# z's norms taken by four rows from slots of their own, and z's statistics, scalings, block sums and w_sp's pieces moved to other chunks

## The chip, the cores and the metric

One core of a Trainium2 chip runs the whole kernel. The metric is the device time of one execution in microseconds (us), as the median of several. Engines are named as in the profile: PE is TensorE's matmul, PEld its weight load, DVE is VectorE, ACT is ScalarE, POOL is GpSimd, SP is SyncE, which only issues transfers (SPq).

## The reference

An FNet layer (two DFTs) and a gMLP layer, each behind a layer norm with a shift, a scale and a gate from `c`. S = 2048 rows, D = 512, half width Fh = 896.

```python
mod = (_silu(c) @ w_mod).reshape(c.shape[0], 6, 1, -1)
sa, ca, ga, sb, cb, gb = (mod[:, 0], ..., mod[:, 5])
h = _layernorm(x) * (1 + ca) + sa
x = x + ga * _A_ref(h, ...)         # y = Re(DFT_seq(DFT_hidden(h)))
h = _layernorm(x) * (1 + cb) + sb
z = _gelu(einsum("bsd,df->bsf", h, w_in))
z1 = z[..., :Fh]
z2 = _layernorm(z[..., Fh:])
g = einsum("ts,bsf->btf", w_sp, z2) + b_sp[None, :, None]
x = x + gb * einsum("bsf,fd->bsd", z1 * g, w_out)
```

## The kernel before

**Arithmetic.** Every fp32 product is made of three matmuls (`matmul3`, L96 to L98): each operand is split into a high part (ACT copies it to fp32r: `ah`, `bh`, `wh`) and a low part (DVE subtracts: `al`, `bl`, `wl`). The large products are done with seven block products instead of eight (the "forms" 1, 2, 6, 7, 4, 5, 3), so sums of blocks of `w_in`, of h and of `w_sp` are made on DVE, and partial results are copied between PSUM banks and SBUF on ACT, or added on DVE, when a form is finished.

**Chunks.** PE's work is a list of chunks, and everything else hangs on their numbers. Five stages matter here; "y+3" is chunk 3 of stage y.

- **y** (`Y0`, 32 chunks of 12 matmuls): the last FNet product. Per row block m, `load_g` brings `gr` from DRAM (SP), `split_g` makes `gh` (ACT, L91) and `gl` (DVE, L92), `seed_y` writes x into the PSUM bank (ACT, L856), `post_y` copies the result out as `x` (ACT, L868), stores it (POOL, `x_d`) and takes its norm; `norm_y` and `post_h` make h and store it (POOL, `h_d`, L880). The tile of `x` has two slots, that of `gr` two.
- **z1** (`N2`, which is also `YE`; 28 chunks, 16 of 12 matmuls and 12 of 9): the left half of z, forms in the order above, two chunks to a form, once for each half of the rows.
- **z2** (`N3`, 28 chunks of 12 matmuls of 448 columns): the right half of z. The first 14 chunks give rows 0 to 7 (of 16 blocks of 128 rows, called rows from here on), the last 14 rows 8 to 15 (`zq`). When form 6, 7, 2 or 4 is done, ACT copies (L1037) or applies gelu (L1039); after forms 5 and 3, DVE adds (L1042) and ACT applies gelu (L1046). Form 3 goes on in the banks that form 5's adds read, and form 7 in those that form 6's copies read, so PE waits for these at once.
- **gw** (`N4`, `NB[p]`): seven products with `w_sp`, 16 chunks each, in the order 1, 6, 7, 4, 5, 3, 2; then the last product, **o**.

**What sets the order.** `at(n, f, ...)` and `atd` enter a call into a table under chunk n; `run(n)` emits what stands there, in order of entry: in y behind the chunk's matmuls, in z1 and z2 ahead of them (and behind `prep(n)`, which makes `al` for chunk n + 2, L272, and `ah` for n + 3, L264), in gw behind them. There is no scheduler: an engine runs its instructions in this order, and one that waits holds up all behind it. SP is not tied to chunks in time, only in order: it issues a load as soon as its slot is free.

**What the change touches.** `stat_z` takes the statistics of one half of a row (DVE, L1059); `norm_z` joins the two halves (DVE, L1063) and takes the reciprocal root and the shift on POOL (L1065 to L1068), in tiles `mvz`, `rsz`, `nmrz` of which there are four slots each; `scale_z` applies them, on DVE for rows 4 to 7 (L1074), on ACT for all others (L120, called from L1076). `hi_w`, `lo_w`, `sum_w` split and sum the blocks of `w_in`'s right half for z2. The 16 pieces of `w_sp` whose block sums are taken ahead: `load_s` brings one (SP, 768 KB in two transfers), `sum_s` makes three sums (DVE, L1099, L1100, L1103), and these go to `s_d` (three stores of 256 KB, by POOL, or in stage y by SP through `store_s`, L1111). `sum_t23(k)` sums blocks of the scaled z (DVE, L1134, L1135) for form 6 of gw.

Of the kernel before, what the change touches and what calls it, by code (L numbers as in the profile page):

```python
# [19 lines left out]
def fnet_gmlp_kernel(  # L20
# [91 lines left out]
    def norm(src, name):
# [902 lines left out]
    def mm_z2(n):  # L1015
        i, c = divmod(n - N3, NP)
        q, p, k = 1 - i, FORMS[c // 2], c % 2
        here, there = (0, 4) if i == 0 else (4, 0)
# [4 lines left out]
        th, tl = AH.pop(n), AL.pop(n)
        wh, wl = WF[1, p]
        for r in range(4):
            ts = slice(r * P, (r + 1) * P)
            matmul3(acc[r][:, :ZH], th[:, ts], tl[:, ts], wh[:, k], wl[:, k], k == 0 and p in (1, 5), k == 1, p not in (1, 5))
        if k == 0:
            return
        ta, tb = [4 * TS[2 * q + j] for j in range(2)]  # L1030
        left, right = slice(0, ZH), slice(ZH, FH)
        for r in range(4):
            if p == 1:
                ZG[r] = bank(there + r, f"z2g{q}_{r}")
                nc.scalar.activation(ZG[r][:, :ZH], ZT[r][:, :ZH], AF.Copy)
            elif p in (6, 7):
                nc.scalar.activation(row_z((ta if p == 6 else tb) + r)[:, right], ZG[r][:, :ZH], AF.Copy)  # L1037
            elif p in (2, 4):
                nc.scalar.activation(row_z((ta if p == 2 else tb) + r)[:, left], acc[r][:, :ZH], AF.Gelu_apprx_tanh)  # L1039
            else:  # L1040
                z = Z[(tb if p == 5 else ta) + r][:, right]
                nc.vector.tensor_tensor(z, ZT[r][:, :ZH], z, op=ALU.add)  # L1042
# [12 lines left out]
    def stat_z(s, h):
        g = s // 8
# [2 lines left out]
        nc.vector.bn_stats(ST[g][:, s % 8, h, :6], Z[s][:, h * ZH:(h + 1) * ZH])  # L1059

    def norm_z(s):
        mv = small.tile([P, 2], F32, tag="mv", name=f"mvz{s}")
        nc.vector.bn_aggr(mv, ST[s // 8][:, s % 8, :, :6])  # L1063
        r = small.tile([P, 1], F32, tag="rs", name=f"rsz{s}")
        nc.gpsimd.tensor_scalar(mv[:, 1:2], mv[:, 1:2], EPS, 1.0, op0=ALU.add, op1=ALU.mult)  # L1065
        nc.gpsimd.tensor_tensor(r, mv[:, 1:2], mhalf, op=ALU.pow)
        nmr = small.tile([P, 1], F32, tag="nmr", name=f"nmrz{s}")
        nc.gpsimd.tensor_scalar(nmr, mv[:, 0:1], r, -1.0, op0=ALU.mult, op1=ALU.mult)  # L1068
# [610 lines left out]
```

## Time and profile before

| | us |
|---|---|
| median of 3 runs (lowest, highest) | 931.78 (931.55, 932.77) |
| the profiled execution | 932.23 |
| its span, first to last instruction | 930.4 |
| PE busy | 917.4 (99%) |
| DVE busy | 759.1 (82%) |
| ACT busy | 447.3 (48%) |
| POOL busy | 153.0 (16%) |
| mean granted TensorE clock | 0.998 |

How to read it: the page gives each engine's busy time and the groups of instructions; the view of waits says which engine waited for which instruction, how long in total, how often, and the longest; a timeline row gives start, duration, engine, line, operation and, in brackets, how long the engine had stood idle and what ended that; windows give an engine's busy time in a stretch, the clock granted to PE and the busy share of the 16 DMA engines. In the profiled execution stage y starts at 343.24 us, z1 at 432.64, z2 at 501.62 and gw at 577.72.

### The profile page before, as it was taken

The numbers are of one execution on the slowest core, as the hardware profiler recorded it, in microseconds if no ns is written. First come the engines' busy times: TensorE is split into PE (matmuls) and PEld (weight loads), VectorE is DVE, ScalarE is ACT, GpSimd is POOL, SyncE is SP. The second block draws the span as 40 slices with busy tenths as digits, with TensorE's granted clock in tenths as the row PEclk, the third lists the DMA queues.
The fourth block names the chain that finished last, engine by engine and source line by source line (L and its number), as shares of the span: only waits on it lengthen the run. The fifth ranks groups of instructions, "written<-read, shape, count | busy, mean of one in ns | idle before, by whom it ended". The sixth has DMA issues, their size and how long they took to land.

```text
span 930.4 us, 12042 instructions
## 1 busy us (share of the span) xinstructions
PE 917.4 (99%) x4040; PEld 759.3 (82%) x4040; DVE 759.1 (82%) x1039; ACT 447.3 (48%) x721; POOL 153.0 (16%) x291
## 2 busy tenths in 40 slices
PE   9999999999999999999999989999999999999998
PEld 6888888888888888877888978888888888888886
DVE  7879789889978885978786877986799789895972
ACT  3585354354354354555777665653554444431221
POOL 1431001100110015745121151500100100000000
PEclk9999999999999999999999999999999999999999
DMA  9999948798864658995783354768878856742641
GB/s 207 225 204 190 223 107 228 190 170 193 226 188 107 181 180 243 339 288 188 228 299 147 118 121 131 219 159 234 218 183 255 220 117 146 192 127 102 210 152 56
DMA packets 261310, 174.62 MB, mean 188 GB/s; under 512 B 134720, under 2 KB 225088, under 8 KB 261120
## 3 DMA queue, kind: packets, MB, share of 16 engines
q1 hardware_dynamic: 246592, 132.16, 57.3%
q0 software_dynamic: 11664, 39.08, 11.2%
q10 hardware_dynamic: 2992, 2.62, 1.2%
q8 instruction: 31, 0.51, 0.2%
q14 instruction: 31, 0.25, 0.1%
HBM read 130.81 MB, written 43.00 MB: 187 GB/s over the span
## 4 chain that ended last, share of the span: by engine, by line
PE 82%; DVE 6%; DMA 5%; issue 3%; ACT 2%; POOL 2%; SPq 0%; ACTq 0%; DVEq 0%; POOLq 0%
PE gw L97 9%; PE gw L98 9%; PE gw L96 9%; PE gs_c L97 3%; PE gs_c L98 3%; PE gs_c L96 3%; PE op L97 3%; PE op L96 3%; PE op L98 3%; PE gp L98 2%; PE gp L633 2%; PE gp L96 2%; PE gp L97 2%; PE gs_u L97 2%; PE gs_u L96 2%
## 5 line engine op out<-in xcount | busy, mean ns | idle before, releaser
L97 PE MATMUL gw<-al,bh 128*128 128x512 f32 x400 | 155.8, 390 | 0.3 <-DVE al L272 0.3
L98 PE MATMUL gw<-ah,bl 128*128 128x512 f32 x400 | 155.7, 389 | 0.0
L96 PE MATMUL gw<-ah,bh 128*128 128x512 f32 x400 | 155.6, 389 | 0.0
L264 ACT ACTIVATE ah<-t 128x512 fp32r<-128x512 f32 x120 | 75.0, 625 | 87.9 <-PE gw L98 46.7
L272 DVE TENSOR_TENSOR al<-t,ah 128x512 fp32r<-128x512 f32 x120 | 81.5, 686 | 37.3 <-PE gw L97 35.0
L97 PEld LDWEIGHTS gw<-al,bh 128*128 128x128 f32 x400 | 75.1, 188 | 16.7 <-DVE al L272 1.2
L98 PEld LDWEIGHTS gw<-ah,bl 128*128 128x128 f32 x400 | 75.1, 188 | 15.6
L96 PEld LDWEIGHTS gw<-ah,bh 128*128 128x128 f32 x400 | 75.1, 188 | 15.5
L231 DVE STREAM_TRANSPOSE t<-stage 128x1024 f32<-128x1024 f32 x56 | 69.4, 1239 | 2.5 <-DMA stage<-in_B_w_sp_dram 2.5
L602 ACT ACTIVATE ph<-f 128x1024 fp32r<-128x1024 f32 x42 | 44.4, 1058 | 40.7 <-PE gs_c L98 17.2
L606 DVE TENSOR_TENSOR pl<-f,ph 128x1024 fp32r<-128x1024 f32 x42 | 50.9, 1215 | 14.0 <-ACT ph L602 13.8
L97 PE MATMUL gs_c<-pl,hh 128*128 128x512 f32 x144 | 56.1, 390 | 0.1
L98 PE MATMUL gs_c<-ph,hl 128*128 128x512 f32 x144 | 56.1, 389 | 0.0
L96 PE MATMUL gs_c<-ph,hh 128*128 128x512 f32 x144 | 56.0, 389 | 0.0
L602 ACT ACTIVATE ph<-tp 128x1024 fp32r<-128x1024 f32 x35 | 36.9, 1054 | 38.3 <-PE gs_v L98 15.9
L606 DVE TENSOR_TENSOR pl<-tp,ph 128x1024 fp32r<-128x1024 f32 x35 | 42.2, 1207 | 7.2 <-ACT ph L602 7.2
L537 DVE STREAM_TRANSPOSE tp<-stage 128x1024 f32<-128x1024 f32 x36 | 44.2, 1230 | 0.2
L96 PE MATMUL op<-woh,uh 128*128 128x512 f32 x112 | 43.6, 389 | 0.0
L97 PE MATMUL op<-wol,uh 128*128 128x512 f32 x112 | 43.6, 389 | 0.0
L98 PE MATMUL op<-woh,ul 128*128 128x512 f32 x112 | 43.6, 389 | 0.0
L1147 ACT ACTIVATE bh<-z 128x512 fp32r<-128x512 f32 (+1 forms) x40 | 23.5, 588 | 40.6 <-PE gw L97 36.6
L1234 ACT ACTIVATE uh<-g 128x512 fp32r<-128x512 f32 x16 | 10.1, 630 | 61.1 <-PE op L97 57.4
(302 smaller groups left out, 2292.7 us busy)
## 6 DMA issues: line engine op xcount, KB each, us to landing
stage<-s_d SPq DMA_DIRECT2D x128, 128.0 KB, 3.0
stage<-in_A_dft_seq_re_dram SPq DMA_DIRECT2D x52, 256.0 KB, 6.5
stage<-in_B_w_sp_dram SPq DMA_DIRECT2D x96, 128.0 KB, 3.3
stage<-in_A_dft_seq_im_dram SPq DMA_DIRECT2D x44, 256.0 KB, 5.3
s_d<-sj POOLq DMA_DIRECT2D x39, 256.0 KB, 3.6
sj<-in_B_w_sp_dram SPq DMA_DIRECT2D x16, 512.0 KB, 6.0
gr<-g_d SPq DMA_DIRECT2D x12, 512.0 KB, 6.8
sb<-in_A_dft_seq_im_dram SPq DMA_DIRECT2D x16, 256.0 KB, 6.0
```

The costliest lines, as they stand in the source:

```text
L96: nc.tensor.matmul(acc, ah, bh, start=first, stop=False, skip_group_check=go_on)
L97: nc.tensor.matmul(acc, ah, bl, start=False, stop=False, skip_group_check=go_on)
L98: nc.tensor.matmul(acc, al, bh, start=False, stop=last, skip_group_check=go_on)
L231: nc.vector.transpose(t.rearrange("p r (b i) -> p r b i", i=32), st[:, :, :, 16 * k:16 * k + 32])
L264: nc.scalar.activation(*parts_z(n, AH), AF.Copy)
L272: nc.vector.tensor_tensor(lo, src_, parts_z(n, AH)[0].bitcast(F32), op=ALU.subtract)
L537: nc.vector.transpose(dst.rearrange("p k (b i) -> p k b i", i=32), st[:, :, 64 * m:64 * m + 64].rearrange("p b (k i) -> p k b i", k=2))
L602: nc.scalar.activation(pair_of(PH, u, "ph"), source_unit(u), AF.Copy)
L606: nc.vector.tensor_tensor(pair_of(PL, u, "pl"), source_unit(u), PH[u].bitcast(F32), op=ALU.subtract)
L633: nc.tensor.matmul(GP[j, k], a[:, k, :], b, start=s == 0 and b is ah and a is h_hi[s], stop=False)
L1147: nc.scalar.activation(BH[p, k][:, :w], b_of(p, k), AF.Copy)
L1234: nc.scalar.activation(UT[t, i][0][:, :4], a, AF.Copy)
```

## The change

No matmul is added, removed or moved. Six things are different:

1. `norm_z` takes four rows at a time. Its tile of four rows by four numbers (mean, variance, root, shift) has the tag `bst`, with four slots, so each of the four groups has its own. Per group there are four joins on DVE, as before, and four POOL instructions on 128x4 instead of twelve on 128x1; the shift is now a product and a negation.
2. `stat_z` runs at n + 3 and n + 4 behind its form's last chunk n (was n + 1, n + 2), except form 2's, which stays in the first half and goes to n + 2, n + 3 in the second; `norm_z` at n + 5 (was n + 2, n + 3); `scale_z` from n + 7 (was n + 6 for rows 4 to 7 and n + 3 for the others).
3. `w_sp`'s pieces: of the three pieces in stage y the last goes to z1; the sums of the nine last pieces run at z1+15, z1+17, z1+21, z2+0, z2+2, z2+7, z2+9, z2+21 and z2+22 (were y+13, z1+15, z1+18, z2+7, z2+9, z2+19, z2+22, gw+2 and gw+5).
4. The sums and splits of `w_in`'s right half run one to three chunks later, from z1+22 on.
5. `sum_t23(k)` runs five chunks later, at gw+8+2k.
6. `mhalf` has four columns.

```diff
     def norm_z(s):
-        mv = small.tile([P, 2], F32, tag="mv", name=f"mvz{s}")
-        nc.vector.bn_aggr(mv, ST[s // 8][:, s % 8, :, :6])
-        r = small.tile([P, 1], F32, tag="rs", name=f"rsz{s}")
-        nc.gpsimd.tensor_scalar(mv[:, 1:2], mv[:, 1:2], EPS, 1.0, op0=ALU.add, op1=ALU.mult)
-        nc.gpsimd.tensor_tensor(r, mv[:, 1:2], mhalf, op=ALU.pow)
-        nmr = small.tile([P, 1], F32, tag="nmr", name=f"nmrz{s}")
-        nc.gpsimd.tensor_scalar(nmr, mv[:, 0:1], r, -1.0, op0=ALU.mult, op1=ALU.mult)
-        ZN[s] = r, nmr
+        m = small.tile([P, 4, 4], F32, tag="bst", name=f"mvz{s}")
+        for r in range(4):
+            nc.vector.bn_aggr(m[:, r, 0:2], ST[s // 8][:, (s + r) % 8, :, :6])
+            ZN[s + r] = m[:, r, 2:3], m[:, r, 3:4]
+        mean, var, rs, nmr = [m[:, :, j] for j in range(4)]
+        nc.gpsimd.tensor_scalar(var, var, EPS, 1.0, op0=ALU.add, op1=ALU.mult)
+        nc.gpsimd.tensor_tensor(rs, var, mhalf, op=ALU.pow)
+        nc.gpsimd.tensor_tensor(nmr, mean, rs, op=ALU.mult)
+        nc.gpsimd.tensor_scalar(nmr, nmr, -1.0, 1.0, op0=ALU.mult, op1=ALU.mult)
...
                 s_, h = (ta if p in (2, 3) else tb) + r, p in (5, 3)
-                at(n + 1 + r // 2, stat_z, s_, h)
+                at(n + (3 if p != 2 else 1 + i) + r // 2, stat_z, s_, h)
                 if h:
-                    at(n + 2 + r // 2, norm_z, s_)
-                    at(n + (3 if i or p == 3 else 6) + r, scale_z, s_, i == 0 and p == 5)
+                    at(n + 7 + r, scale_z, s_, i == 0 and p == 5)
+            if h:
+                at(n + 5, norm_z, s_ - 3)
...
-    early += tuple((Y0 + n, Y0 + m) for n, m in ((3, 6), (4, 8), (9, 13)))
-    early += tuple((YE + n, YE + m) for n, m in ((9, 15), (13, 18), (30, 35), (32, 37), (42, 47), (45, 50), (51, 58), (55, 61)))
+    early += tuple((Y0 + n, Y0 + m) for n, m in ((3, 6), (4, 8)))
+    early += tuple((YE + n, YE + m) for n, m in ((9, 15), (12, 17), (17, 21), (20, 28), (24, 30), (31, 35), (33, 37), (39, 49), (41, 50)))
...
-                     (18, (hi_w, 1, 2)), (19, (lo_w, 1, 2)), (20, (hi_w, 1, 1)), (21, (lo_w, 1, 1)), (22, (sum_w, 1, 5)),
-                     (23, (sum_w, 1, 6), (hi_w, 1, 6)), (24, (lo_w, 1, 6)), (25, (sum_w, 1, 7)), (26, (hi_w, 1, 7)), (27, (lo_w, 1, 7)),
-                     (28, (sum_w, 1, 4)), (29, (hi_w, 1, 4)), (30, (lo_w, 1, 4)), (31, (hi_w, 1, 5)), (32, (lo_w, 1, 5)), (33, (hi_w, 1, 3)),
-                     (34, (lo_w, 1, 3))):
+                     (18, (hi_w, 1, 2)), (19, (lo_w, 1, 2)), (20, (hi_w, 1, 1)), (22, (lo_w, 1, 1)), (23, (sum_w, 1, 5)),
+                     (24, (sum_w, 1, 6), (hi_w, 1, 6)), (26, (lo_w, 1, 6)), (27, (sum_w, 1, 7), (hi_w, 1, 7)), (29, (lo_w, 1, 7)),
+                     (31, (sum_w, 1, 4)), (32, (hi_w, 1, 4)), (33, (lo_w, 1, 4), (hi_w, 1, 5)), (34, (lo_w, 1, 5)), (35, (hi_w, 1, 3)),
+                     (36, (lo_w, 1, 3))):
...
-                at(n + 3, sum_t23, k)
+                at(n + 8, sum_t23, k)
```

Three places in the order of the instructions matter below. The first is ACT's order in the second half of z2, from form 1's copies (z2+15) to form 7's (z2+21); `ah` is a high part for PE, `zq` is z's rows 8 to 15, `z_0` to `z_3` are rows 0 to 3, and L120 is their scaling. Before:

```order
L1035 ACTIVATE z2g_3_4907<-z2p_1_3_4856 128x448
L264 ACTIVATE ah_4911<-hs_3763 128x4x4x32
L120 ACTIVATE z_0_4580<-z_0_4580,nmrz_4878,rsz_4875 128x896
L264 ACTIVATE ah_4942<-hz_3739 128x4x4x32
L120 ACTIVATE z_1_4582<-z_1_4582,nmrz_4885,rsz_4882 128x896
L1039 ACTIVATE zq<-z2p_1_0_4853 128x448
...
L264 ACTIVATE ah_4967<-hz_3739 128x4x4x32
L120 ACTIVATE z_2_4584<-z_2_4584,nmrz_4919,rsz_4916 128x896
L264 ACTIVATE ah_4997<-hz_3739 128x4x4x32
L120 ACTIVATE z_3_4586<-z_3_4586,nmrz_4926,rsz_4923 128x896
L1037 ACTIVATE zq<-z2g_0_4901 128x448
```

And now:

```order
L1035 ACTIVATE z2g_3_4882<-z2p_1_3_4845 128x448
L264 ACTIVATE ah_4886<-hs_3754 128x4x4x32
L264 ACTIVATE ah_4913<-hz_3730 128x4x4x32
L1039 ACTIVATE zq<-z2p_1_0_4842 128x448
...
L264 ACTIVATE ah_4935<-hz_3730 128x4x4x32
L264 ACTIVATE ah_4970<-hz_3730 128x4x4x32
L1037 ACTIVATE zq<-z2g_0_4876 128x448
...
L264 ACTIVATE ah_4994<-hz_3730 128x4x4x32
L120 ACTIVATE z_0_4592<-z_0_4592,mvz_4947 128x896
L264 ACTIVATE ah_5023<-hs_3751 128x4x4x32
L120 ACTIVATE z_1_4594<-z_1_4594,mvz_4947 128x896
```

The four scalings stood ahead of form 6's copies (L1037), two of them ahead of form 2's gelus (L1039); now the first stands behind form 6's copies.

The second place is DVE's order at the end of z1, about the adds of the second half's form 5 (L997, `z1k_7`; they free the banks in which form 3 goes on): `wl_6` is a low part of `w_in` for form 6 of z2, `wraw` the block sum for form 7. Before:

```order
L949 TENSOR_TENSOR wt_4387<-wraw_2_4167,wraw_0_4084 128x896
L272 TENSOR_TENSOR al_4410<-zq,ah_4385 128x512
L964 TENSOR_TENSOR wl_6_4390<-wt_4387,wh_6_4389 128x896
L272 TENSOR_TENSOR al_4427<-zq,ah_4412 128x512
L949 TENSOR_TENSOR wraw_0_4084<-wraw_2_4167,wraw_0_4084 128x2x448
L997 TENSOR_TENSOR z1k_7_0_4360<-z1p_5_0_4415,z1k_7_0_4360 128x512
```

And now:

```order
L949 TENSOR_TENSOR wt_4415<-wraw_2_4158,wraw_0_4075 128x896
L272 TENSOR_TENSOR al_4432<-zq,ah_4410 128x512
L997 TENSOR_TENSOR z1k_7_0_4360<-z1p_5_0_4420,z1k_7_0_4360 128x512
L997 TENSOR_TENSOR z1k_7_1_4362<-z1p_5_1_4421,z1k_7_1_4362 128x512
L997 TENSOR_TENSOR z1k_7_2_4364<-z1p_5_2_4422,z1k_7_2_4364 128x512
L272 TENSOR_TENSOR al_4454<-zq,ah_4434 128x4x4x32
L964 TENSOR_TENSOR wl_6_4418<-wt_4415,wh_6_4417 128x896
L272 TENSOR_TENSOR al_4468<-zq,ah_4456 128x4x4x32
L949 TENSOR_TENSOR wraw_0_4075<-wraw_2_4158,wraw_0_4075 128x2x448
```

`wl_6` and form 7's sum stood ahead of the adds and now stand behind them.

The third place is SP's queue in the second half of stage y: `sj` is a piece of `w_sp`, `stage<-h_d` the first load for z1. Before:

```order
L847 DMA xr_3397<-in_A_x_dram 128x512
L1111 DMA s_d_10_98<-sj_3238 128x512
L1111 DMA s_d_10_102<-sj_3238 128x512
L1111 DMA s_d_10_106<-sj_3238 128x512
L165 DMA stage_3419<-h_d_91 32x16x128 x4
L843 DMA gr_3427<-g_d_76 128x8x128
```

And now:

```order
L843 DMA gr_3360<-g_d_76 128x8x128
L847 DMA xr_3391<-in_A_x_dram 128x512
L165 DMA stage_3410<-h_d_91 32x16x128 x4
L843 DMA gr_3418<-g_d_76 128x8x128
L847 DMA xr_3448<-in_A_x_dram 128x512
```

The three stores of the third piece are gone from the queue ahead of `stage<-h_d` and the next `gr`, as are its two loads some rows earlier.

More of the change, by code (lines that the diff above doesn't have):

```diff
@@ L108, in stats @@
         nc.gpsimd.tensor_scalar(mv[:, 1:2], mv[:, 1:2], EPS, 1.0, op0=ALU.add, op1=ALU.mult)
-        nc.gpsimd.tensor_tensor(r, mv[:, 1:2], mhalf, op=ALU.pow)
+        nc.gpsimd.tensor_tensor(r, mv[:, 1:2], mhalf[:, 0:1], op=ALU.pow)
         return mv[:, 0:1], r
@@ L290, in fnet_gmlp_kernel @@
     ccol = cpool.tile([P, ND], F32, name="ccol")
-    mhalf = cpool.tile([P, 1], F32, name="mhalf")
+    mhalf = cpool.tile([P, 4], F32, name="mhalf")
     nc.gpsimd.memset(mhalf, -0.5)
@@ L404, in stats_first @@
         nc.vector.tensor_scalar(mv[:, 1:2], mv[:, 1:2], EPS, None, op0=ALU.add)
-        nc.gpsimd.tensor_tensor(mv[:, 2:3], mv[:, 1:2], mhalf, op=ALU.pow)
+        nc.gpsimd.tensor_tensor(mv[:, 2:3], mv[:, 1:2], mhalf[:, 0:1], op=ALU.pow)
         NRM[s] = mv[:, 0:1], mv[:, 2:3]
@@ L431, in square_x @@
         nc.gpsimd.tensor_scalar(m[:, 1:2], m[:, 1:2], 1.0 / D, EPS, op0=ALU.mult, op1=ALU.add)
-        nc.gpsimd.tensor_tensor(m[:, 2:3], m[:, 1:2], mhalf, op=ALU.pow)
+        nc.gpsimd.tensor_tensor(m[:, 2:3], m[:, 1:2], mhalf[:, 0:1], op=ALU.pow)
         nc.gpsimd.tensor_tensor(m[:, 3:4], m[:, 0:1], m[:, 2:3], op=ALU.mult)
@@ L1061, in norm_z @@
     def norm_z(s):
-        mv = small.tile([P, 2], F32, tag="mv", name=f"mvz{s}")
-        nc.vector.bn_aggr(mv, ST[s // 8][:, s % 8, :, :6])
-        r = small.tile([P, 1], F32, tag="rs", name=f"rsz{s}")
-        nc.gpsimd.tensor_scalar(mv[:, 1:2], mv[:, 1:2], EPS, 1.0, op0=ALU.add, op1=ALU.mult)
-        nc.gpsimd.tensor_tensor(r, mv[:, 1:2], mhalf, op=ALU.pow)
-        nmr = small.tile([P, 1], F32, tag="nmr", name=f"nmrz{s}")
-        nc.gpsimd.tensor_scalar(nmr, mv[:, 0:1], r, -1.0, op0=ALU.mult, op1=ALU.mult)
-        ZN[s] = r, nmr
+        m = small.tile([P, 4, 4], F32, tag="bst", name=f"mvz{s}")
[7 more added lines that the diff above has]
+        nc.gpsimd.tensor_scalar(nmr, nmr, -1.0, 1.0, op0=ALU.mult, op1=ALU.mult)
     def scale_z(s, on_vector):
@@ L1472, in load_gelu @@
     def load_gelu():
-        nc.scalar.activation(ccol[:, 0:1], mhalf, AF.Gelu_apprx_tanh)
+        nc.scalar.activation(ccol[:, 0:1], mhalf[:, 0:1], AF.Gelu_apprx_tanh)
     wstack = ctx.enter_context(ExitStack())
```

## The prediction

> **What bounds the kernel now.** First the page's line of busy times, then windows over the four stages that are edited (length, busy time and count of each engine, PEclk as the granted clock, DMA share), with one window from within stage y and one behind PE's longest wait.
>
> ```profile
> PE 917.4 (99%) x4040; PEld 759.3 (82%) x4040; DVE 759.1 (82%) x1039; ACT 447.3 (48%) x721; POOL 153.0 (16%) x291
> ```
>
> ```profile
> 343.20:432.60 89.40, 87.89 (x385) 71.86 (x384) 68.64 (x97) 46.41 (x66) 43.65 (x64) 1.00 0.86 262
> 432.60:501.60 69.00, 68.30 (x301) 56.25 (x301) 53.17 (x75) 48.54 (x82) 20.80 (x36) 1.00 0.75 252
> 501.60:577.70 76.10, 70.84 (x337) 64.07 (x336) 58.32 (x102) 51.59 (x93) 18.15 (x39) 0.98 0.37 113
> 577.70:665.30 87.60, 87.28 (x385) 71.95 (x385) 71.42 (x109) 44.90 (x73) 17.91 (x35) 1.00 0.77 209
> ...
> 379.00:391.00 12.00, 12.00 (x54) 9.94 (x54) 11.72 (x17) 6.55 (x9) 9.23 (x11) 1.00 1.05 367
> ...
> 555.30:558.80 3.50, 3.45 (x10) 3.09 (x10) 2.75 (x5) 1.82 (x4) 1.94 (x3) 0.52 0.35 144
> ```
>
> PE is the bound, and the matmuls stay the same, so only time that PE loses can be won. Where it is undisturbed (379 to 391), 53 matmuls start in 12.00 us (the window counts one more at its border), 0.2265 each: a chunk of twelve is 2.72 us, one of nine 2.04. Stage y should then last 32 x 2.72 = 87.0 and lasts 89.4 (2.4 lost); z1 16 x 2.72 + 12 x 2.04 = 68.0 of 69.0 (1.0 lost); gw's first two products 32 x 2.72 = 87.0 of 87.6 (0.6 lost). For z2 I take PE's timeline:
>
> ```profile
> 550.88 0.37 PE L98 MATMUL z2g<-wh,al 128*128 128x448 f32 x1
> 555.35 0.74 PE L96 MATMUL z2g<-wh,ah 128*128 128x448 f32 x1 [4.10 <-ACT zq L1037]
> ...
> 559.40 0.37 PE L96 MATMUL z2g<-wh,ah 128*128 128x448 f32 x1
> ...
> 561.84 0.36 PE L96 MATMUL z2g<-wh,ah 128*128 128x448 f32 x1
> ```
>
> The chunk z2+21, from 559.40 to 561.84, is undisturbed: 2.44. 28 x 2.44 = 68.3 of 76.1: 7.8 lost. Together **11.8 us** can be won, no more. PE's view of waits (us in total, times, longest) names the places:
>
> ```profile
> PE z2g L96 <- ACT zq L1037: 4.1, 1, 4.1
> PE yp L96 <- ACT yp L856: 1.5, 2, 0.8
> ...
> PE z2p L96 <- DVE zq L1042: 1.1, 1, 1.1
> PE z1p L96 <- DVE z1k L997: 0.7, 1, 0.7
> PE gw L97 <- DVE al L272: 0.3, 1, 0.3
> ```
>
> **The norms in z2: 5.9 us.** The timeline of the engines ahead of the long wait:
>
> ```profile
> 543.92 0.69 DVE L272 TENSOR_TENSOR al<-hs,ah 128x512 fp32r<-128x512 f32 x1 [1.14 <-PE z2p L98]
> 544.53 0.74 DVE L1074 TENSOR_SCALAR z<-z,rsz,nmrz 128x896 f32<-128x896 f32 x1
> ...
> 545.42 0.55 POOL L1066 TENSOR_TENSOR rsz<-mvz,mhalf 128x1 f32<-128x1 f32 x1 [2.61 <-DVE z L1074]
> ...
> 546.38 1.14 ACT L120 ACTIVATE z<-z,nmrz,rsz 128x896 f32<-128x896 f32 x1 [3.94 <-POOL nmrz L1068]
> ...
> 554.75 1.85 ACT L1037 ACTIVATE zq<-z2g 128x448 f32<-128x448 f32 x4
> 556.45 0.68 ACT L264 ACTIVATE ah<-hz 128x512 fp32r<-128x512 f32 x1
> ...
> 578.13 0.27 DVE L1063 BATCH_NORM_AGGREGATE mvz<-st 128x2 f32<-128x12 f32 x2
> ```
>
> `rsz` has four slots. The fifth row's root waits 2.61 on POOL until DVE has scaled the first row (L1074), which stands at z2+17 behind an `al` that itself waits for PE. ACT's scaling of `z_0` stands 3.94 behind that, and the gelus and copies behind it come late, so PE stands from 550.88 + 0.20 to 555.35 (4.3 lost); its next chunk takes 559.40 - 555.35 = 4.05 instead of 2.44 (1.6 more), at the granted clock 0.52 of the window from 555.3. With a slot per group no root waits for a scaling, and `z_0` to `z_3` stand behind form 6's copies: 5.9 gone. Late next is the new chain on POOL:
>
> ```profile
> L1066 POOL TENSOR_TENSOR rsz<-mvz,mhalf x16: 549/550/1000, 535.4 to 595.5; 128x1 f32<-128x1 f32 x16
> ...
> L1068 POOL TENSOR_SCALAR nmrz<-mvz,rsz x16: 267/268/804, 536.0 to 596.5; 128x1 f32<-128x1 f32 x16
> ...
> L1065 POOL TENSOR_SCALAR mvz<-mvz x16: 183/187/637, 535.1 to 594.8; 128x1 f32<-128x1 f32 x16
> ```
>
> (ns: least, median, most.) No row shows 128x4. At best four instructions cost medians: 0.19 + 0.55 + 0.27 + 0.27 = 1.3 us; at worst four times the slowest, 4 x (0.64 + 1.00 + 0.80 + 0.80) = 13.0. I take 1.3, the rows nearest in size. The room: DVE makes the four joins (0.54) at z2+18 behind `al` (0.69) and a scaling (0.74), so at 2.0 after that chunk's start. ACT runs form 6's copies from 0.6 into z2+19, when its first block is done, to 2.5, then an `ah` (0.68): it comes to `z_0` 0.7 into z2+20. Two scalings and an `ah` more (3.0) bring it to 1.3 into z2+21, and form 7's first copy (1.85 / 4) to 1.8 of 2.44: 0.6 to spare. 2 x 2.44 + 0.7 - 2.0 + 0.6 = 4.2 against 1.3: hidden.
>
> On the price of a rest: the rows show 1.6 us lost to the clock behind an idle of 4.3. In proportion, an idle of 2.2 would cost another 0.8. [...]
>
> **Form 5's adds: 1.4 us.** The same timeline, later:
>
> ```profile
> 562.72 0.68 DVE L1099 TENSOR_TENSOR sj<-sj 128x512 f32<-128x512 f32 x1
> ...
> 567.58 1.24 DVE L231 STREAM_TRANSPOSE t<-stage 128x1024 f32<-128x1024 f32 x1
> 568.74 0.65 DVE L1152 TENSOR_TENSOR bl<-z,bh 128x512 fp32r<-128x512 f32 x1
> ...
> 570.96 1.15 DVE L1059 BATCH_NORM_STATS2 st<-zq 128x6 f32<-128x448 f32 x2
> 572.02 2.20 DVE L1042 TENSOR_TENSOR zq<-z2p,zq 128x448 f32<-128x448 f32 x4
> ```
>
> Two pairs of statistics (1.15 each) stand ahead of the adds for which PE waits 1.1. They go behind, and at z2+25 DVE has only one `al` first: 1.1 gone. What is left of z2's loss, 7.8 - 5.9 - 1.1 = 0.8, has no row of its own; form 5's adds of the first half meet the same statistics, and I take 0.3 for them: 1.4 of 1.9.
>
> What they meet there: z2+26 then holds `al`, a transpose, `bl` and two statistics, 0.69 + 1.24 + 0.65 + 1.15 = 3.7 in 2.44 us; z2+27 1.8 and the adds' 2.2; gw+0 3.7 of 2.72; gw+1 1.8; gw+2 4.3 with the joins; gw+3 1.8. From 0.7 behind at z2+26, DVE finishes gw+3's `al` (for gw+5) at 0.7 + 3.7 + 4.0 + 3.7 + 1.8 + 4.3 + 0.7 = 18.9 after z2+26's start; PE wants it at 2 x 2.44 + 5 x 2.72 = 18.5. Rows overlap their neighbours by about 0.1, over some 20 rows 2 us. So between 0.4 late and 1.6 early; I cost 0.2. Of gw's own loss, 0.6, the cause goes:
>
> ```profile
> 589.36 1.14 ACT L120 ACTIVATE zq<-zq,nmrz,rsz 128x896 f32<-128x896 f32 x1 [2.05 <-POOL nmrz L1068]
> ...
> 591.35 0.64 DVE L272 TENSOR_TENSOR al<-t,ah 128x512 fp32r<-128x512 f32 x1
> ```
>
> ACT waits 2.05 for one row's shift, `bh`, `bl` and that `al` queue behind it; two pieces' sums (3 x 0.68 each) and `sum_t23` stood there too and are gone, to z2+21 and 22 (where `al`, scaling and sums make 3.5 and 2.7 in 2.44, and z2+23 has one `al` to catch up) and to gw+8, three chunks (8.2 us) before its reader. Net 0.6 - 0.2 = 0.4.
>
> **z1's adds: 0.9 us.**
>
> ```profile
> 495.59 1.08 DVE L949 TENSOR_TENSOR wraw<-wraw,wraw 128x896 f32<-128x896 f32 x1
> 496.59 1.88 DVE L997 TENSOR_TENSOR z1k<-z1p,z1k 128x512 f32<-128x512 f32 x3
> ```
>
> That sum and `wl_6` no longer stand ahead of the adds: 0.9 of 1.0. The weights come 1 to 3 chunks later, the last low part at z2+8 for z2+12. A piece's sums at z2+0 and at z2+2 add 2.1 each to chunks with 1 to 2 us of DVE work: nothing, or the whole 0.9 back if they make form 1's successors late.
>
> **Stage y: 2.0 us.**
>
> ```profile
> 386.19 1.75 SPq L1111 DMA_DIRECT2D s_d<-sj  x3
> 388.17 4.12 SPq L165 DMA_DIRECT2D stage<-h_d  x4
> 392.39 1.83 SPq L843 DMA_DIRECT2D gr<-g_d  x1
> ...
> 401.10 1.06 ACT L91 ACTIVATE gh<-gr 128x1024 fp32r<-128x1024 f32 x1 [3.89 <-DMA gr<-g_d]
> ...
> 420.48 0.60 ACT L868 ACTIVATE x<-yp 128x512 f32<-128x512 f32 x1 [0.90 <-DMA x_d<-x]
> ```
>
> ACT waits 3.89 for the `gr` issued at 392.39, behind 1 MB of `h_d` and the third piece's stores, on DMA engines at a share of 1.05. What hangs on it (`gh`, `gl`, a transpose, `h_d`, and POOL's `x_d` behind `h_d`) makes both seeds late for which PE waits (1.5, with the chunks around 2.4). Without the stores SP is 388.17 - 386.19 = 2.0 earlier, and 0.79 MB less at 367 GB/s are 2.1 more: `gr` lands 2.0 to 4.1 earlier, and each of PE's waits is under 1.0. I take 2.0 of 2.4, from ends of 0 and 2.4. The piece's traffic moves to z1, where the DMA share is 0.75.
>
> **Sum.** 5.9 + 1.4 + 0.4 + 0.9 + 2.0 = 10.6. On the profiled execution, 932.2 (its span of 930.4 and 1.8 around it), that gives 921.6; the median of the 3 runs, 931.8, lies 0.4 lower, so the forecast for a median is **921.2**.
>
> **The rivals.**
> - *Stage y keeps its waits* (11%). For: of the 4.4 MB of the window from 379 (12.0 x 367 GB/s) only 0.8 go, so the engines stay busy at 0.86, and `x_d`, for which ACT waits until 420.4, may land as late as now. Against: the queue's 2.0. Time 921.2 + 2.0 = 923.2.
> - *DVE becomes the bound around gw+3* (8%): the overlap of rows isn't there and `bl` waits for `bh`; 0.4 late becomes a chunk's excess, 4.3 - 2.7 = 1.6, and z1's 0.9 returns through the new sums. Time 923.7.
> - *The change does half of what it says* (5%): `z_0` still meets an unfinished chain, or `z_4` on DVE, which stands only two chunks behind its joins; half of the 4.3 stays, 2.2 to 3.0 with the clock. Time 923.4 to 924.2.
> - *Slower: the chain on POOL is long* (4%). With a chain of c us, PE waits c - 4.2 in z2, plus 1.6 for the clock, and again at gw+4, where ACT works three chunks ahead (8.2) and one scaling takes 1.1 of that, c - 7.0. At c = 13.0: 8.8 + 1.6 + 6.0 = 16.4, so 937.6. It has eaten the gain when 2c - 11.2 + 1.6 = 10.6, at c = 10.1. For: POOL's rows already differ threefold for one size. Against: none of the 48 takes over 1.00.
>
> **How the numbers follow.** The forecast has 72% (920.0 to 922.8). The least possible is 931.8 - 11.8 = 920.0, with 0.2 for scatter 919.8. At the other end, rivals of one sign may come together, the first two 921.2 + 2.0 + 2.5 = 925.7; I say 919.8 to 925.7, which leaves out the slow case and mixtures. 0.2% (1.9 us) is about what a measurement of this kernel can tell from no change: faster 0.91, same 0.04, slower 0.05 (the slow case and 0.01 for what I don't see).
>
> **What would show it.** Right: no wait of PE for L1037 near z2+20 and a granted clock of 1.00 there, POOL's four instructions at 1.3 to 3 us a group and no idle of ACT ahead of L120 over 1; no statistics between `al` and L1042; ACT's wait for `gr` under 2 and stage y in 87.0 to 87.8. Wrong: an L120 or a scaling on DVE that waits for `mvz`; waits of PE for `al` at gw+3 to gw+6; a wait of DVE for `sj` in z1; the y seeds late as before.

## The result and the profile after

The changed kernel takes **921.28 us** (median of 5 runs, 920.77 to 923.21), the kernel before beside it 932.28 (5 runs, 931.55 to 934.34). The ratio is 0.9884, 95% interval 0.9867 to 0.9900: 11.0 us faster, where 10.6 were forecast. The profiled execution has a span of 919.1 (before 930.4).

First the page's line of busy times, then the windows over the four edited stages, cut at each stage's first matmul, and PE's view of waits (us in total, times, longest), in which one row is left; that wait lies at the start of the program, outside the four stages.

```profile
PE 913.8 (99%) x4040; PEld 758.8 (83%) x4040; DVE 759.8 (83%) x1039; ACT 450.0 (49%) x721; POOL 137.8 (15%) x262
```

```profile
343.72:430.76 87.04, 87.04 (x385) 72.07 (x384) 67.79 (x97) 46.38 (x66) 41.90 (x66) 1.00 0.82 252
430.76:498.76 68.00, 68.00 (x301) 56.31 (x300) 52.83 (x74) 48.53 (x81) 20.55 (x37) 1.00 0.79 262
498.76:566.86 68.10, 68.10 (x338) 63.10 (x337) 61.89 (x106) 52.91 (x94) 15.67 (x29) 1.00 0.55 177
566.86:653.92 87.06, 87.06 (x386) 72.10 (x385) 68.93 (x106) 45.45 (x73) 7.66 (x13) 1.00 0.69 181
```

```profile
PE busyp L353 <- DVE busy L296: 1.4, 1, 1.4
```

In all four stages PE is busy for the whole length at a clock of 1.00. Against the starts of before (343.24, 432.64, 501.62, 577.72), y is 89.40 - 87.04 = 2.4 shorter, z1 1.0, z2 8.0 and gw's two products 0.6: 12.0 us, all that PE lost there. The span gains 11.3: stage y starts 0.5 later, at 343.72 instead of 343.24, and what follows the four stages takes 0.2 longer.

The timeline around the long wait of before, now without one:

```profile
544.07 0.41 DVE L1065 BATCH_NORM_AGGREGATE mvz<-st 128x2 f32<-128x12 f32 x4
...
544.57 0.20 POOL L1068 TENSOR_SCALAR mvz<-mvz 128x4 f32<-128x4 f32 x1 [3.15 <-DVE mvz L1065]
...
544.86 1.03 POOL L1069 TENSOR_TENSOR mvz<-mvz,mhalf 128x4 f32<-128x4 f32 x1
...
545.96 0.69 POOL L1070 TENSOR_TENSOR mvz<-mvz 128x4 f32<-128x4 f32 x1
...
546.74 0.20 POOL L1071 TENSOR_SCALAR mvz<-mvz 128x4 f32<-128x4 f32 x1
...
548.57 1.13 ACT L120 ACTIVATE z<-z,mvz 128x896 f32<-128x896 f32 x1
...
560.44 2.38 DVE L1042 TENSOR_TENSOR zq<-z2p,zq 128x448 f32<-128x448 f32 x4
...
565.07 1.14 DVE L1060 BATCH_NORM_STATS2 st<-zq 128x6 f32<-128x448 f32 x2
...
579.70 1.14 ACT L120 ACTIVATE zq<-zq,mvz 128x896 f32<-128x896 f32 x1 [0.81 <-POOL mvz L1071]
...
588.68 0.69 DVE L272 TENSOR_TENSOR al<-t,ah 128x512 fp32r<-128x512 f32 x1 [2.03 <-PE gw L97]
```

POOL's chain for `z_0` to `z_3` runs from 544.57 to 546.94, 2.37 us, and ACT comes to `z_0` (no brackets: it waits for nothing) 1.63 later. Form 5's adds (560.44) stand ahead of the statistics (565.07). One ACT scaling in gw waits 0.81 for its shift, and by gw+8 DVE is early enough to wait for PE (2.03).

### The profile page after: what moved, and what is told of

Its sections match the earlier page's. It is cut to its first block, busy times and chain, and to the rows that moved or that the text cites. A ratio compares the mean times of both kernels' runs of the same rounds, so it can differ in the third digit from the quotient of the medians.

```text
span 919.1 us, 11985 instructions
## 1 busy us (share of the span) xinstructions
PE 913.8 (99%) x4040; PEld 758.8 (83%) x4040; DVE 759.8 (83%) x1039; ACT 450.0 (49%) x721; POOL 137.8 (15%) x262
## 4 chain that ended last, share of the span: by engine, by line
PE 94%; DVE 2%; DMA 1%; ACT 1%; issue 1%; POOL 0%; ACTq 0%; SPq 0%; DVEq 0%
PE gw L97 10%; PE gw L96 10%; PE gw L98 10%; PE gs_c L97 4%; PE gs_c L98 4%; PE gs_c L96 4%; PE yp L97 3%; PE yp L98 3%; PE yp L96 3%; PE op L98 3%; PE op L97 3%; PE op L96 3%; PE gs_u L98 3%; PE gs_u L97 3%; PE gs_u L96 3%; PE gp L98 2%
## 5 line engine op out<-in xcount | busy, mean ns | idle before, releaser
L1236 ACT ACTIVATE uh<-g 128x512 fp32r<-128x512 f32 x16 | 10.1, 631 | 61.1 <-PE op L97 57.3
```

The lines of the kernel that those rows point to most:

```text
L1236: nc.scalar.activation(UT[t, i][0][:, :4], a, AF.Copy)
```

## The experiments

Twelve kernels ran, each beside the kernel before on the same chip. Where nothing else is said, one is the changed kernel with one edit. The ratio is to the kernel before, with its 95% interval; the last four columns are what PE loses in each stage of the profiled execution, over undisturbed chunks of 2.72, 2.04 and (z2) 2.433 us, added up from PE's timeline.

| kernel | median us | ratio | y | z1 | z2 | gw |
|---|---|---|---|---|---|---|
| before | 932.28 | 1 | 2.4 | 1.0 | 8.0 | 0.6 |
| changed | 921.28 | 0.9884 (0.9867 to 0.9900) | 0 | 0 | 0 | 0 |
| slots_only | 924.00 | 0.9919 (0.9904 to 0.9934) | 0 | 0 | 3.1 | 0 |
| chunks_only | 920.81 | 0.9884 (0.9870 to 0.9899) | 0 | 0 | 0 | 0 |
| norms_as_before | 928.80 | 0.9967 (0.9957 to 0.9977) | 0 | 0 | 8.9 | 0 |
| by_row_own | 920.79 | 0.9885 (0.9870 to 0.9899) | 0 | 0 | 0 | 0 |
| stats_back | 923.08 | 0.9907 (0.9892 to 0.9921) | 0.7 | 0 | 2.2 | 0 |
| piece_in_y | 921.68 | 0.9891 (0.9877 to 0.9906) | 0.9 | 0 | 0 | 0 |
| y_two | 927.67 | 0.9960 (0.9945 to 0.9975) | 6.8 | 0 | 0 | 0 |
| before_again | 931.77 | 1.0003 (0.9993 to 1.0012) | 1.0 | 1.0 | 7.9 | 0.7 |
| w_sums_back | 926.68 | 0.9946 (0.9931 to 0.9961) | 0 | 4.3 | 1.2 | 0 |
| gw_back | 922.61 | 0.9902 (0.9886 to 0.9919) | 0 | 0 | 0 | 1.8 |
| pool_14 | 927.69 | 0.9955 (0.9939 to 0.9972) | 0 | 0 | 6.7 | 0 |
| pool_24 | 930.28 | 0.9983 (0.9974 to 0.9992) | 1.2 | 0 | 9.5 | 0 |

### Slots or chunks

Four kernels separate the two things that the prediction named in one breath for z2's 5.9 us: slots of their own for the norms, and later places for them. `slots_only` has the old places, one row at a time, in one tile for four rows:

```diff
-                at(n + (3 if p != 2 else 1 + i) + r // 2, stat_z, s_, h)
+                at(n + 1 + r // 2, stat_z, s_, h)
...
-                    at(n + 7 + r, scale_z, s_, i == 0 and p == 5)
-            if h:
-                at(n + 5, norm_z, s_ - 3)
+                    at(n + 2 + r // 2, norm_z, s_)
+                    at(n + (3 if i or p == 3 else 6) + r, scale_z, s_, i == 0 and p == 5)
...
+        if s % 4 == 0:
+            MZ[0] = small.tile([P, 4, 4], F32, tag="bst", name=f"mvz{s}")
+        m = MZ[0][:, s % 4]
```

> The changed kernel with z's statistics, norms and scalings back at the chunks of before, the norms one row at a time, but in slots of their own (one tile for four rows instead of the ring of four). Theory 'ring': the slots alone free z_0's scaling, so the 5.9 us stay won and only the 1.4 to 1.9 of the statistics ahead of form 5's adds come back: PE waits for L1042 near z2+25 and nowhere for L1037, 922.7 to 923.2 us. Rival 'chunks': the old places of the scalings are what holds ACT, and the wait at z2+20 comes back with the clock: 927 to 929 us.

`chunks_only` keeps the new places, with the `norm_z` of before (tags `mv`, `rs`, `nmr`, four slots each):

```diff
                 if h:
+                    at(n + 5, norm_z, s_)
                     at(n + 7 + r, scale_z, s_, i == 0 and p == 5)
-            if h:
-                at(n + 5, norm_z, s_ - 3)
```

> The changed kernel with the ring of four slots and the norms one row at a time, at the new chunks. Theory 'ring' as the prediction put it: the fifth root still waits for the first scaling, so part of the 5.9 us comes back, 923.5 to 927 us. Rival 'either is enough': at the new chunks the first scaling on DVE (z_4 at z2+18) stands just behind z_0's join and each further one 2.4 us on, while ACT wants z_0 only 4 us later: POOL waits up to 3 us in front of a root, ACT waits for none of them, and PE loses nothing: 921.3 us within 0.5.

`norms_as_before` has both as before, `by_row_own` neither (new places, own slots, but three POOL instructions of 128x1 for each row).

> The changed kernel with statistics, norms (ring of four, one row at a time) and scalings all as before; the pieces of w_sp, sum_t23 and the block sums as changed. If the terms of the prediction add: 5.9 + 1.4 (at most 1.9) come back, 928.6 to 929.1 us, with PE's wait of about 4 us for L1037 at z2+20 and a granted clock of about 0.5 behind it. Rival 'the terms overlap': the moved sums of w_sp in z2+20 to 24 change the backlog of DVE, and the loss is 1 us or more away from 7.3.

> The changed kernel with slots of its own for each group, at the new chunks, but norms one row at a time on POOL: twelve instructions of 128x1 a group instead of four of 128x4. Theory 'four at a time buys nothing here': a group takes 4 x (0.19 + 0.55 + 0.27) = 4.0 us and more, but z_0's shift is there after the first 1.0, so no wait; 921.3 us within 0.5. Rival: POOL's 4 us of a group hold the last rows or the stores behind them, and ACT or DVE waits: up to 1 us more.

PE's waits in `norms_as_before` and in `slots_only`:

```profile
PE z2g L96 <- ACT zq L1037: 4.1, 1, 4.1
...
PE z2p L96 <- DVE zq L1042: 1.1, 1, 1.1
```

```profile
PE z2p L96 <- DVE zq L1042: 1.1, 1, 1.1
PE z2g L96 <- ACT zq L1037: 0.9, 1, 0.9
```

What the norms cost with both as before, by the timeline at z2+19 to z2+21, is 4.30 + 2.21 + 0.44 = 6.95 us. Own slots at the old places leave 1.10 + 0.10 = 1.20 of it; the new places with the old ring leave nothing, and so does one row at a time. So the ring was the cause at the old places, but **the new places alone are enough**, and the four-row norms and their slots buy no time there. The rival "either is enough" is right for the chunks; slots alone are not quite enough. What stays in `slots_only` is again ACT's order: its four scalings stand ahead of form 6's copies, and the first waits for POOL, which begins with its row only at 539.33, behind the four rows of the other group:

```profile
540.55 1.14 ACT L120 ACTIVATE z<-z,mvz 128x896 f32<-128x896 f32 x1 [1.41 <-POOL mvz L1070]
```

Neither "5.9 stay won" nor "the wait comes back" was met exactly: 924.0 lies between the two theories (923.2 and 927). `norms_as_before` at 928.8 is what the sum of the two terms said (928.6 to 929.1).

### The statistics alone

```diff
-                at(n + (3 if p != 2 else 1 + i) + r // 2, stat_z, s_, h)
+                at(n + 1 + r // 2, stat_z, s_, h)
```

> The changed kernel with z's statistics alone back at the chunks of before (norms by four in their own slots, scalings as changed). The prediction's term: form 5's adds lose 1.1 in the second half (z2+25) and 0.3 in the first, so 1.4 us come back: 922.7 us, PE waits for L1042. Rival: z2's rest of 0.8 without a row belongs to them too: 1.9, 923.2 us. Second rival: without scalings in front, DVE has room and nothing comes back: 921.3.

```profile
560.96 1.14 DVE L1060 BATCH_NORM_STATS2 st<-zq 128x6 f32<-128x448 f32 x2
562.01 0.68 DVE L272 TENSOR_TENSOR al<-hs,ah 128x512 fp32r<-128x512 f32 x1
562.61 1.15 DVE L1060 BATCH_NORM_STATS2 st<-zq 128x6 f32<-128x448 f32 x2
563.67 2.20 DVE L1042 TENSOR_TENSOR zq<-z2p,zq 128x448 f32<-128x448 f32 x4
```

The picture of before is back: two pairs of statistics, then the adds for which PE waits 1.0. z2 loses 2.2: 1.17 + 0.07 at z2+25 and 26, 0.26 + 0.12 at z2+11 and 12, and 12 x 0.046 in the chunks between, where nothing waits. For these the windows over the four chunks from z2+14, in before and in the changed kernel:

```profile
536.21:546.13 9.92, 9.92 (x49) 9.01 (x48) 7.88 (x19) 5.67 (x11) 4.95 (x13) 1.00 1.00 213
```

```profile
532.81:542.54 9.73, 9.73 (x50) 9.02 (x49) 8.81 (x20) 7.90 (x15) 2.12 (x4) 1.00 0.93 217
```

Behind the short wait at z2+12, 48 matmuls take 9.92 us instead of 9.73 (206.7 ns each instead of 202.7), at a granted clock of 1.00, and PE goes on so until its next wait: to z2+18 in before (2.48 a chunk), to z2+24 in `stats_back` (9.92 from 538.50 to 548.42). In the changed kernel, with no wait, it never happens (its 28 chunks take 2.43 to 2.44 each). That is part of z2's rest for which the prediction had no row. The first rival (1.9) is the nearest; the second falls.

### The piece of w_sp in stage y

```diff
-    early += tuple((Y0 + n, Y0 + m) for n, m in ((3, 6), (4, 8)))
+    early += tuple((Y0 + n, Y0 + m) for n, m in ((3, 6), (4, 8), (9, 13)))
-    early += tuple((YE + n, YE + m) for n, m in ((9, 15), (12, 17), ...
+    early += tuple((YE + n, YE + m) for n, m in ((12, 17), ...
```

> The changed kernel with the third piece of w_sp back in stage y (loaded at chunk 9, stored at 15 as before), the pieces behind it as changed. The prediction's term: 2.0 us (at most 2.4) come back, ACT waits 3 to 4 us for gr, PE waits for the seeds, y takes 89.0 to 89.4: 923.3 to 923.7 us. Rival: the waits of before came from the engines' load of that one execution and the piece is nearly free: under 0.7 us.

ACT's wait for `gr` in `piece_in_y`:

```profile
400.69 1.06 ACT L91 ACTIVATE gh<-gr 128x1024 fp32r<-128x1024 f32 x1 [4.08 <-DMA gr<-g_d]
```

y loses 0.9, not 2.0. The wait of ACT for `gr` that the theory named is there (4.08), but PE waits only 0.3. Since two kernels without the piece (`stats_back` and `pool_24`) had lost 0.7 and 1.2 in y, two more runs asked whether the piece matters at all: `y_two` puts a second one there besides (loaded at y+14, summed at y+18; the two pieces loaded at y+3 and y+4 stand in every kernel), and `before_again` is the kernel before, unchanged.

> The changed kernel with two pieces of w_sp in stage y instead of none (loaded at chunks 9 and 14, stored at 15 and 20); with one of them it lost 0.8 us in y by its profile. Theory 'the traffic of the piece is what y waits for': twice the traffic beside the same h_d, gr and x_d makes the seeds later, y loses 2 to 4 us, 923 to 925 us. Rival 'y's waits come and go': kernels without any piece there have lost 0.7 and 1.2 us in single executions too, so the loss stays under 1.2 and the time at 921 to 922.2 us.

> The kernel of before once more, for a second profiled execution of the same program. Theory 'the losses belong to the program': z2's wait of 4.1 us at z2+20, z1's 0.9 to 1.0 and gw's 0.6 come again within 0.1. [...] y's 2.4, made of waits for DMAs, comes again only if it is not chance: rival 0 to 1.2. Time 931 to 933 us.

First PE's waits of `y_two`, then the wait of its ACT:

```profile
PE yp L96 <- ACT yp L856: 2.7, 1, 2.7
```

```profile
404.07 1.06 ACT L91 ACTIVATE gh<-gr 128x1024 fp32r<-128x1024 f32 x1 [7.71 <-DMA gr<-g_d]
```

```profile
343.76:431.80 88.04, 87.65 (x386) 71.89 (x385) 68.35 (x97) 46.01 (x66) 42.62 (x64) 1.00 0.86 265
```

The last row is stage y of `before_again`, with a little over its end: the first matmul of z1 starts at 431.78, so y takes 88.02 and loses 1.0. So the traffic is the cause: two pieces make ACT wait 7.71 and cost 6.8, more than either theory said. Of this, 2.9 are one rest of PE, and 3.0 were lost behind it at a granted clock of 0.50, from 405.40 to 412.22 (the last section has windows). Whether the traffic acts through the load of the DMA engines or through the order of SP's queue, no run separates: the `gr` that ACT waits for was issued at 393.94 here and at 388.52 in the changed kernel. The size of the loss differs from one execution to the next: with one piece 2.4, 1.0 and 0.9 (mean 1.4), without it 0 in eight of the ten profiled kernels and 0.7 and 1.2 in two (mean 0.2). By these few profiles a piece is worth some 1.2 us, and 2.4 was a high draw; by the medians it is less, `piece_in_y` being 0.4 us above the changed kernel and 0.9 above `chunks_only`. z1, z2 and gw lost the same in both executions of before (1.0, 7.9 to 8.0, 0.6 to 0.7), and behind the rest at z2+20 1.67 were lost, as 1.62 had been.

### w_in's sums, and gw

`w_sums_back` has `hi_w`, `lo_w` and `sum_w` at the chunks of before, `gw_back` these:

```diff
-                at(n + 8, sum_t23, k)
+                at(n + 3, sum_t23, k)
...
-    ... (33, 37), (39, 49), (41, 50)))
+    ... (33, 37), (51, 58), (55, 61)))
```

> The changed kernel with z2's weights (sum_w, hi_w, lo_w) at the chunks of before. The prediction's term: 0.9 us comes back, at z1+25 and z1+26, with L949's sum and wl ahead of form 5's adds: 922.2 us. Rival: sum and low part slide, since the pieces of w_sp there moved too: under 0.3, or with the pieces' sums at z1+21 on top over 1.5.

The timelines of DVE and of ACT in `w_sums_back`, and PE's waits:

```profile
485.32 0.69 DVE L1101 TENSOR_TENSOR sj<-sj 128x512 f32<-128x512 f32 x1 [1.27 <-DMA sj<-in_B_w_sp_dram]
...
495.03 0.69 DVE L272 TENSOR_TENSOR al<-zq,ah 128x512 fp32r<-128x512 f32 x1 [1.37 <-ACT ah L264]
495.64 1.08 DVE L949 TENSOR_TENSOR wraw<-wraw,wraw 128x896 f32<-128x896 f32 x1
496.64 1.88 DVE L997 TENSOR_TENSOR z1k<-z1p,z1k 128x512 f32<-128x512 f32 x3
```

```profile
491.58 0.96 ACT L961 ACTIVATE wh<-wt 128x896 fp32r<-128x896 f32 x1 [2.67 <-DVE wt L949]
492.44 2.04 ACT L1005 ACTIVATE z<-z1g 128x512 f32<-128x512 f32 x4
```

```profile
PE z1p L96 <- DVE z1k L997: 2.4, 1, 2.4
...
PE z2p L96 <- ACT z2g L1035: 1.0, 1, 1.0
```

5.5 us come back, not 0.9. The piece whose sums now stand at z1+21 puts a wait of 1.27 and three sums of 0.69 ahead of the sum `wt`; at its old place `wh` then holds ACT for 2.67, form 4's copies (L1005) follow at 492.44 (488.76 in the changed kernel), an `ah` and an `al` behind them, and form 5's adds come last. So the two tables are **one edit**: the pieces could go to z1 without a loss only because the sums of `w_in` moved too. In the kernel before, without a piece at z1+21, the same places cost 1.0. That the piece at z1+21 is what makes the difference is read from the timelines; no run takes out that piece alone.

> The changed kernel with sum_t23 back at three chunks behind its product's start and the last two pieces of w_sp back at gw+2 and gw+5. The prediction's term: 0.4 to 0.6 us comes back around gw+5. Rival 'DVE is the bound there': with the statistics at gw+0 to gw+3 the low part for gw+5 is only 1.4 us early, 2.0 of sums and 1.1 of sum_t23 go ahead of it, so 1.7 us are lost: 923.0 us.

The rows of PE's timeline in `gw_back` that wait:

```profile
581.42 0.50 PE L97 MATMUL gw<-al,bh 128*128 128x512 f32 x1 [0.53 <-DVE al L272]
...
590.49 0.50 PE L97 MATMUL gw<-al,bh 128*128 128x512 f32 x1 [0.58 <-DVE al L272]
```

These waits cost 1.8 us, the rival's size, at gw+5 and gw+8. The low part for gw+5 in `gw_back`, and the same one in the changed kernel:

```profile
580.69 0.68 DVE L272 TENSOR_TENSOR al<-t,ah 128x512 fp32r<-128x512 f32 x1
```

```profile
578.61 0.67 DVE L272 TENSOR_TENSOR al<-t,ah 128x512 fp32r<-128x512 f32 x1
```

It ends at 581.37 here and at 579.28 in the changed kernel, 2.1 later by one piece's three sums. PE wants it 0.23 into gw+5, which in the changed kernel is 580.48 + 0.23 = 580.71: 1.4 early. The prediction had said between 0.4 late and 1.6 early. Ahead of the low part for gw+8 stand the other piece's sums and two calls of `sum_t23` as well.

### A longer chain on POOL

```diff
+        for _ in range(14 if s == 0 else 0):
+            nc.gpsimd.tensor_scalar(nmr, nmr, 1.0, 1.0, op0=ALU.mult, op1=ALU.mult)
         nc.gpsimd.tensor_scalar(nmr, nmr, -1.0, 1.0, op0=ALU.mult, op1=ALU.mult)
```

> The changed kernel with 14 more POOL multiplications by 1.0 (128x4) in the chain of the group z_0 to z_3 alone. By the pitch of the rows of 128x4 (0.20 + 0.09 to the next) the chain of 2.4 us grows by 4.1 to 6.5. The prediction's room is 4.2, so PE waits 6.5 - 4.2 = 2.3 us in z2+21 or 22, with a granted clock of 1.00 behind it if the clock goes down only after a longer idle time: 923.6 us. Rival 'in proportion': 0.9 more for the clock, 924.5. Second rival: ACT's backlog is not made good and PE loses the whole 4.1 or more: 925.4.

> The same with 24 more multiplications: the chain grows by 7.0 to 9.4 us, PE waits 9.4 - 4.2 = 5.2 and then loses 1.6 to a granted clock of about 0.5 for a chunk: 928.1 us. Rival: the room is smaller or larger than 4.2 by what this run and the one with 14 show in common (their difference, 2.9 us of chain, is then the same in PE's time plus the clock's 1.6).

The timelines of POOL, ACT and PE in each:

```profile
546.47 6.17 POOL L1072 TENSOR_SCALAR mvz<-mvz 128x4 f32<-128x4 f32 x14
...
553.33 1.13 ACT L120 ACTIVATE z<-z,mvz 128x896 f32<-128x896 f32 x1 [4.93 <-POOL mvz L1073]
...
556.49 0.74 PE L96 MATMUL z2g<-wh,ah 128*128 128x448 f32 x1 [4.33 <-ACT zq L1037]
```

```profile
547.75 9.38 POOL L1072 TENSOR_SCALAR mvz<-mvz 128x4 f32<-128x4 f32 x24
...
560.61 0.74 PE L96 MATMUL z2g<-wh,ah 128*128 128x448 f32 x1 [7.17 <-ACT zq L1037]
```

The chains are 544.30 to 553.30 = 9.0 us and 545.59 to 557.42 = 11.8: the multiplications, each of which reads what the one before wrote, took 0.44 and 0.39 on average, not 0.29 (the last section has their spread). So PE's waits are longer than expected, and the times are 927.7 and 930.3 instead of 923.6 and 928.1. They still give the room. The chunk in which PE waits is 4.49 and 7.33 too long, and 9.0 - 4.49 = 4.5, 11.8 - 7.33 = 4.5. **The room is 4.5 us**, where the prediction had worked out 4.2, and beyond it each microsecond of the chain is one of PE's. Behind the waits 2.2 and 1.9 more are lost at a granted clock of 0.50 (554.30 to 561.12 with 14, 557.75 to 564.57 with 24): nothing had been expected with 14, and it is not in proportion either.

## Why the prediction was right

**The sum.** 10.6 forecast, 11.0 by the medians. By the terms, 8.0 in z2 (forecast 7.3), 1.0 in z1 (0.9), 0.6 in gw (0.4) and some 1.2 in y (2.0): 10.8. The forecast case held: no wait of PE took the place of one removed. That the sum came out this close is in part luck: z2, z1 and gw together gave 1.0 more than forecast, and y some 0.8 less.

**The norms in z2, 5.9.** Size and place hold (4.31 + 1.62 in before; 4.40 + 1.67 in `before_again`). The cause was given as the ring of four, with the new places beside it; the runs show that at the new places the ring costs nothing, and that with its slots alone 1.2 us would have stayed. That half of the step would have misled an engineer who wanted the smallest edit: `chunks_only`, which keeps the norms of before, has it at 920.8.

**Form 5's adds, 1.4 of z2's other 1.9.** All the rest of z2 was won, 2.0 to 2.1, 0.6 more than forecast: 1.28 in the second half (forecast 1.1, the wait alone without what the chunks around it lose), 0.37 in the first (0.3), and 0.3 from the slower matmuls between and 0.1 at z2+2, which no step had.

**The POOL chain, 1.3.** Mis-sized: 2.37 us, and 2.9 for the last group in gw. The root of 128x4 takes 1.03 to 1.34 where 128x1 took 0.55, and the product up to 0.69 where 0.27 was assumed; the values were medians of rows of 128x1, the nearest size, and that failed. The room covered it (4.2 forecast, 4.5 measured), so the time was right all the same. The slow rival would have needed 10.1.

**gw, 0.4.** Its parts were 0.6 won and 0.2 given back to a DVE that is late at gw+5; DVE was 1.4 early, inside the range given, so 0.6 stayed. `gw_back` shows that the two pieces and `sum_t23`, which it put back together, had to leave for it.

**z1's adds, 0.9.** Right at 1.0, but the bounds were not: a DVE wait for `sj` was named as a sign of failure, and it is there in the changed kernel (1.62 at 485.46) without costing anything, because `hi_w` and `sum_w` stand later now. That the two moves depend on each other, at 5.5 us, no step said.

**Stage y, 2.0 of 2.4.** The mechanism is right (ACT's waits for `gr` are two of 2.2 in all, as forecast below 2 each; y takes 87.04), the size was not: a mean of 1.4 with the piece and 0.2 without. The step took one execution's waits for DMAs as the program's. The rival "y keeps its waits" was partly true: they come and go without the piece too.

**The price of a rest.** The prediction set a cost in proportion, 0.8 for an idle of 2.2, from the 1.6 behind 4.3. The lower end of its rival's 2.2 to 3.0 is an idle of 2.2 at no price of the clock; that was the author's estimate, and no run shows it. What the runs showed is not in proportion: a rest of 2.6 cost 1.7 more (`w_sums_back`, granted clock 0.50 for 3.41 us), and one of 7.3 cost 1.9 (`pool_24`, 0.50 for 6.82). Behind the wait of 1.1 at z2+25 of before the clock was 1.00.

## What to carry to other kernels

Where a wait hangs on a ring of slots, look first at when its users run: moving them behind what the bound engine wants next can free the ring without a slot more. Moves of several tables are one edit where they share an engine; undo each from the *changed* kernel before you credit it, since its price there (5.5 us here) can be far from what the kernel before lost at the same place (1.0). A loss that is made of waits for DMAs needs more than one profiled execution to be sized (y lost 2.4 and 1.0 in the two of before); losses made of an engine's order came out the same within 0.1 there.

## What the runs showed of the hardware

**A granted clock of 0.50 came behind windows in which PE did little.** In before the clock stands at 0.50 from 555.27 to 558.69, 3.42 us. Windows as long as that, cut where the clock changes, from `w_sums_back`, `pool_24`, `norms_as_before` and `y_two`; the first number behind the length is PE's busy time, and the third from the right the granted clock:

```profile
494.85:498.26 3.41, 0.98 (x5) 0.68 (x5) 3.23 (x5) 1.56 (x4) 0.68 (x1) 1.00 0.93 270
498.26:501.67 3.41, 3.41 (x10) 2.67 (x9) 1.88 (x4) 2.87 (x5) 1.62 (x3) 0.50 1.01 412
501.67:505.09 3.42, 3.42 (x18) 3.00 (x17) 3.42 (x6) 2.15 (x5) 1.08 (x2) 1.00 0.18 73
```

```profile
550.92:554.33 3.41, 2.52 (x13) 1.99 (x11) 3.32 (x6) 0.00 (x0) 2.92 (x7) 1.00 0.00 0
554.33:557.75 3.42, 0.00 (x0) 0.00 (x0) 0.19 (x1) 0.30 (x1) 2.31 (x12) 1.00 0.00 0
557.75:561.16 3.41, 0.55 (x2) 0.51 (x3) 1.99 (x3) 3.41 (x6) 2.10 (x4) 0.50 0.58 231
```

```profile
551.20:554.61 3.41, 2.18 (x6) 1.96 (x7) 1.88 (x4) 3.00 (x6) 0.00 (x0) 0.50 0.00 0
554.61:558.03 3.42, 3.42 (x11) 3.03 (x10) 0.66 (x2) 0.63 (x1) 0.00 (x0) 0.50 0.00 0
```

```profile
401.99:405.40 3.41, 1.44 (x7) 0.86 (x5) 0.24 (x1) 1.33 (x2) 0.00 (x0) 1.00 1.06 368
405.40:408.81 3.41, 2.66 (x6) 2.15 (x7) 3.41 (x4) 1.07 (x3) 0.00 (x0) 0.50 0.33 94
```

At a clock of 1.00, the window with PE busy for 2.52 is followed by one at 1.00, those with 1.44, 0.98 and 0.00 by one at 0.50. At 0.50, the windows with 2.18, with 2.66 (`y_two`) and with 0.55 (`pool_24`) are followed by another at 0.50, those with 3.41 (`w_sums_back`) and 3.42 (`norms_as_before`) by one at 1.00. So the clock stood at 0.50 for 3.41 us in `w_sums_back`, and for 6.82 to 6.83 in the other three. A rest of 2.6 us (from 0.23 behind the last matmul's start to the next) cost 1.7 more in `w_sums_back`, and a rest of 7.3 cost 1.9 in `pool_24`. The same rest of 4.3 cost 1.6 in before, where the clock fell 0.1 ahead of its end, and 2.65 in `norms_as_before`, where it fell at 551.20, 1.2 ahead of the next matmul, and stayed at 0.50 until 558.03. What sets the moment at which the clock changes was not shown.

**POOL's small operations were slow beside some of DVE's.** The same product of 128x4 took 0.20 to 0.69 in the four groups of one execution, and the root 1.03 to 1.34. This is not chance: `pool_14` and `pool_24` repeat the first three durations of the group `z_0` to `z_3` (0.20, 1.03, 0.69) within 0.01. The 14 multiplications in `pool_14` took 0.20 at the least and in the median and 0.64 at most. In the traces of before and of the changed kernel, wherever an instruction of these chains other than the root took over 0.33 (nine in before, four in the changed kernel), DVE was in a TENSOR_TENSOR or a TENSOR_SCALAR during 0.44 or more of it; not every one beside such an instruction was slow (0.27 in before). What the two engines share there, no run shows.

**Matmuls of 448 columns had two paces** at a granted clock of 1.00, 202.7 and 206.7 ns, and in before the pace changed at waits of PE: its chunks take 2.48 from z2+13, behind the short wait at z2+12, to z2+18, and 2.43 to 2.44 from z2+21 on, behind the long wait at z2+20. It need not change: behind the wait at z2+25 the chunk z2+27 takes 2.43 again. The cause stays open.
